# A fused attention and two-layer MoE kernel: token blocks of 512 and 384 in the first MoE layer, and spills of converted weights on POOL's queue

## The chip, the cores and the metric

The kernel runs on one core of a Trainium2 chip. The metric is device time in microseconds (us) of one execution, the median of several runs; lower is better. A core has five engines that run side by side and each work through their own list of instructions in order: TensorE (PE in the profile; its weight loads are shown as PEld), VectorE (DVE), ScalarE (ACT), GpSimd (POOL) and SyncE (SP). SP and POOL also ask for DMA transfers; each does that from its own queue, in the order of its list. Matmuls write to PSUM, eight banks of 512 float32 columns on 128 partitions; everything else lies in SBUF or, if it does not fit, in DRAM.

## What is computed

Softmax attention with a soft cap, then two feed-forward layers over 1792 tokens of width 768. Cut to what matters here:

```python
x = attention(q, k, v, cap)           # 4 x 12 heads x 448 x 64 -> 1792 x 768
h = x @ w_in                          # first layer, 768 x 2048
g = h - np.tanh(h)
y = g @ w_out                         # 2048 x 768
h = y @ w_in2                         # second layer, 768 x 1024
e = np.exp(h - h.max(-1)); solu = h * e / (e.sum(-1) + 1e-9)
out = layer_norm(solu) * g_ln @ w_out2
```

The weights arrive as float64. A weight w is used as a pair of float32r numbers, hi and lo, and so are the activations; a product is three matmuls: hi by hi, hi by lo, lo by hi.

## The kernel before

The tokens are worked on in two halves of 896 (two batches of 448; `hb` 0 and 1). Each half runs attention, then the first MoE layer (`moe1`), then the second (`moe2`). Features lie on partitions and tokens along the free axis, so a half is 896 columns; a PSUM tile has two banks, and the kernel puts 448 columns in each (`hp[:, g, :S]`, g = 0 and 1).

`moe1` has four chunks of 512 hidden features. For each chunk `up` makes four hp tiles of 128 features, from two weight loads of three units; each hp tile takes 6 slices of the input width, 3 products and 2 token groups: 36 matmuls. The very first chunk is made by `first`, which does three of its four tiles group by group (`gg=(g,)`), so that it can begin before the second group's attention is done. `nonlinear` then computes h - tanh(h) on ScalarE and VectorE over all 896 columns: L487, L489, L495, L491 and L501 on ScalarE; L493, L497, L496, L498 and L502 on VectorE. L496 is the last to read hp; L502 makes gl, the lo part of the result. `down` multiplies the chunk with w_out: six op tiles of 24 matmuls (4 slices, 3 products, 2 groups), which are added to `acc` (L524; the first chunk is copied by L522). After the last chunk, L526 and L527 make the hi and lo parts yh and yl, the next layer's input. The order on TensorE is up of chunk c + 1, then down of chunk c. hp and op have two PSUM tiles each, so an hp tile's matmuls wait for L496 of the hp tile two before it, and an op tile's for the add of the op tile two before it.

A weight unit is 128 x 512 weights. In the first half it is loaded as pairs of 32-bit words into one of three `st` buffers (L106, SP's queue), packed by L111, L112 and L113 on VectorE, and split into hi (L119, ScalarE) and lo (L120, or L126 in the second layer, VectorE). The pair stays in one of 13 buffers `w` (and one `wx`) until its matmuls are done. It is also saved to DRAM (`keep`, L136), five units after its conversion, and the second half reads it back (L191, SP's queue; the first 13 by L153 on POOL's) instead of converting again. `keep` is called from `unit`, and at the end of attention and of the second layer's loads for all that are pending.

Attention's order is written out by hand. In the MoE layers a scheduler sets the order on each engine at build time, from priorities and its own estimate of times; once built it is fixed.

Of the kernel before, what the change touches and what calls it, by code (L numbers as in the profile page):

```python
# [9 lines left out]
F32 = mybir.dt.float32  # L10
# [4 lines left out]
ALU = mybir.AluOpType  # L15
# [14 lines left out]
def fused_kernel(ctx, tc, qk_in, v, cap, w1, w2, w3, w4, gln, out):  # L30
    nc = tc.nc
    B, H, S, D = 4, 12, 448, 64
# [6 lines left out]
    NK = DM // P  # L39
    HB = B // 2  # L40
    HT = HB * S
# [7 lines left out]
    NCHUNK = w2.shape[0] // NK  # L49
# [83 lines left out]
    def keep():  # L133
        key, w = pending.pop(0)
        d = drw.tile([P, 2, 512], F32R, name=f"d{key}")
        nc.sync.dma_start(d.bitcast(F32), w.bitcast(F32))  # L136
        saved[key] = d

    ahead = {}
# [307 lines left out]
    def moe1(mp, xh, xl, yh, yl):  # L447
        acc = [mp.tile([P, HT], F32, tag=f"acc{d}", name=f"acc{d}", bufs=1) for d in range(NK)]
        gs = {}
        place.update(pool=(mp, WX1), at=-1)  # L450

        def up_mms(hp, wt, m, k0, k1, gg=(0, 1)):
            ms = slice(m * P, (m + 1) * P)
            for kk in range(k0, k1):
                wh, wl = wt[kk]
                xs = [(xh[kk][:, g * S:(g + 1) * S], xl[kk][:, g * S:(g + 1) * S]) for g in range(2)]
                for i in range(2):
                    for g in gg:
                        nc.tensor.matmul(hp[:, g, :S], wh[:, ms], xs[g][i], start=(kk == 0 and i == 0), stop=False)  # L459
                for g in gg:  # L460
                    nc.tensor.matmul(hp[:, g, :S], wl[:, ms], xs[g][0], start=False, stop=(kk == NK - 1))  # L461

        def first():

            gs[0] = []
            wts = [load_w1(0, 0), load_w1(0, 1)]
            hps = [pst("hp", "ab"[half]) for half in range(2) for _ in range(2)]
            for g, k0, k1 in ((0, 0, NK), (1, 0, 3), (1, 3, 4), (1, 4, 5), (1, 5, 6)):
                for m in range(3):
                    up_mms(hps[m], wts[m // 2], m % 2, k0, k1, (g,))  # L470
                    if k1 == NK and g == 1:
                        nonlinear(0, hps[m])
            up_mms(hps[3], wts[1], 1, 0, NK)
            nonlinear(0, hps[3])

        def up(c, half):
            gs.setdefault(c, [])
            wt = load_w1(c, half)
            for m in range(2):
                hp = pst("hp", "a")  # L480
                up_mms(hp, wt, m, 0, NK)
                nonlinear(c, hp)

        def nonlinear(c, hp):
            h = hp[:, :, :S]
            u = mp.tile([P, 2, S], F32, tag="u", name="u")
            nc.scalar.activation(u, h, AF.Square)  # L487
            t = mp.tile([P, 2, S], F32, tag="t", name="t")
            nc.scalar.activation(t, h, AF.Tanh)  # L489
            mk = mp.tile([P, 2, S], U8, tag="mk", name="mk")  # L490
            nc.scalar.activation(mk, t, AF.Square, scale=TS)  # L491
            gf = mp.tile([P, 2, S], F32, tag="gf", name="gf")
            nc.vector.scalar_tensor_tensor(gf, u, C2, h, ALU.mult, ALU.mult)  # L493
            w = mp.tile([P, 2, S], F32, tag="w", name="w", bufs=1)
            nc.scalar.activation(w, u, AF.Square, bias=gat)  # L495
            nc.vector.tensor_tensor(t, h, t, ALU.subtract)  # L496
            nc.vector.scalar_tensor_tensor(gf, w, GB, gf, ALU.add, ALU.mult)  # L497
            nc.vector.copy_predicated(gf, mk, t)  # L498
            gh = mp.tile([P, 2, S], F32R, tag="gh", name="gh", bufs=6)
            gl = mp.tile([P, 2, S], F32R, tag="gl", name="gl", bufs=6)  # L500
            nc.scalar.copy(gh, gf)  # L501
            nc.vector.tensor_tensor(gl, gf, gh.bitcast(F32), ALU.subtract)  # L502
            gs[c].append((gh, gl))

        def down(c):
            for d in range(NK):
                wt = load_w2(c, d)
                op = pst("op")
                nm = CH // P
                for m in range(nm):  # L510
                    gg = gs[c][m]
                    wh, wl = wt[m]
                    for i in range(2):
                        for g in range(2):
                            nc.tensor.matmul(op[:, g, :S], wh, gg[i][:, g], start=(m == 0 and i == 0), stop=False)  # L515
                    for g in range(2):
                        nc.tensor.matmul(op[:, g, :S], wl, gg[0][:, g], start=False, stop=(m == nm - 1))  # L517
                for g in range(2):
                    cs = slice(g * S, (g + 1) * S)
                    a = acc[d][:, cs]  # L520
                    if c == 0:
                        nc.scalar.copy(a, op[:, g, :S])  # L522
                    else:
                        nc.vector.tensor_tensor(a, op[:, g, :S], a, ALU.add)  # L524
                    if c == NCHUNK - 1:
                        nc.scalar.copy(yh[d][:, cs], a)  # L526
                        nc.vector.tensor_tensor(yl[d][:, cs], a, yh[d][:, cs].bitcast(F32), ALU.subtract)  # L527

        first()
        for c in range(NCHUNK):  # L530
# [151 lines left out]
    for hb in range(2):  # L682
        xh, xl = xtiles()
# [73 lines left out]
```

## Time and profile before

| | |
|---|---|
| Median of 3 runs | 907.37 us (906.84 to 908.77) |
| The profiled execution | 907.26 us, of which the span from first to last instruction is 905.5 us |
| TensorE busy | 897.6 us (99% of the span), 5162 matmuls; weight loads 727.9 us |
| VectorE busy | 613.4 us (68%) |
| ScalarE busy | 416.7 us (46%) |
| GpSimd busy | 48.1 us (5%) |
| DMA | 142.98 MB, mean 158 GB/s; SP's queue 112.95 MB, POOL's 29.20 MB |
| First layer, first half / second half | about 93 to 336 us / about 538 to 780 us |

The granted TensorE clock is 1.00 in every stretch read here. Matmuls are pipelined: the record of one overlaps that of the next, so a group's mean duration is not the time that one adds. That is read from start to start. Shares of the whole span hide that the two halves differ: only the first converts weights.

### The profile page before, as it was taken

How to read it: one execution, taken by the hardware profiler on the slowest of the kernel's cores; microseconds unless marked ns; L12 is line 12 of the kernel's file. 1: busy time of each engine (PE TensorE's matmuls, PEld its weight loads, DVE VectorE, ACT ScalarE, POOL GpSimd, SP SyncE). 2: the span in 40 equal slices, each digit the busy share in tenths (PEclk: the TensorE clock that was granted, in tenths of full speed). 3: DMA queues.
4: the chain of work that ended last, by engine and by line, in shares of the span. 5: the costliest groups of instructions: out<-in, count | busy, mean ns of one | idle time of the engine just before them, and what ended most of it. 6: DMA issues, size and time to landing. Idle time of an engine off the chain costs nothing.

```text
span 905.5 us, 12979 instructions
## 1 busy us (share of the span) xinstructions
PE 897.6 (99%) x5162; PEld 727.9 (80%) x5162; DVE 613.4 (68%) x954; ACT 416.7 (46%) x469; POOL 48.1 (5%) x88
## 2 busy tenths in 40 slices
PE   8999999999999999999999999999999999999998
PEld 5444699999989998888865448999999999888887
DVE  6687989899999990988257985970543634306841
ACT  7999276446254231443279871852512502113311
POOL 2211000000000000001022200000000000000000
PEclk9999999999999999999999999999999999999999
DMA  8554680796875873730256623433242432231301
GB/s 292 183 181 149 229 324 24 237 343 210 268 267 177 320 244 126 255 134 36 102 184 198 209 92 116 134 107 113 73 140 71 138 99 87 70 131 33 128 35 53
DMA packets 46424, 142.98 MB, mean 158 GB/s; under 512 B 10460, under 2 KB 13532, under 8 KB 46364
## 3 DMA queue, kind: packets, MB, share of 16 engines
q1 hardware_dynamic: 39180, 112.95, 36.6%
q0 software_dynamic: 7040, 29.20, 9.4%
q8 instruction: 41, 0.67, 0.3%
q14 instruction: 19, 0.16, 0.1%
q10 hardware_dynamic: 144, 0.00, 0.0%
HBM read 98.64 MB, written 43.33 MB: 157 GB/s over the span
## 4 chain that ended last, share of the span: by engine, by line
PE 84%; DVE 10%; DMA 3%; issue 1%; ACT 1%; SPq 0%; DVEq 0%
PE op L515 14%; PE hp L459 14%; PE op L517 7%; PE hp L461 7%; PE o L307 7%; PE hp L226 4%; PE hp L227 4%; PE hp L225 4%; PE s L275 4%; PE oab L615 2%; PE oab L619 2%; PE oab L616 2%; PE so L324 2%; DMA st<-in_moe_w_out_dram 2%; PE x L281 2%; PE tp L564 1%
## 5 line engine op out<-in xcount | busy, mean ns | idle before, releaser
L459 PE MATMUL hp<-xh,w 128*128 128x448 f32 x384 | 115.8, 368 | 1.5 <-DVE t L496 1.5
L459 PE MATMUL hp<-xl,w 128*128 128x448 f32 x384 | 115.8, 367 | 0.0
L461 PE MATMUL hp<-xh,w 128*128 128x448 f32 x384 | 115.7, 367 | 0.0
L517 PE MATMUL op<-gh,w 128*128 128x448 f32 x336 | 96.4, 367 | 0.0
L515 PE MATMUL op<-gl,w 128*128 128x448 f32 x336 | 96.1, 367 | 0.0
L515 PE MATMUL op<-gh,w 128*128 128x448 f32 x336 | 96.1, 367 | 0.0
L459 PEld LDWEIGHTS hp<-xh,w 128*128 128x128 f32 x384 | 71.8, 188 | 10.5 <-issue 2.5
L461 PEld LDWEIGHTS hp<-xh,w 128*128 128x128 f32 x384 | 72.1, 188 | 7.4 <-issue 0.7
L459 PEld LDWEIGHTS hp<-xl,w 128*128 128x128 f32 x384 | 72.1, 188 | 7.4 <-issue 0.7
L307 PE MATMUL o<-t,vf 128*32 128x448 f32 x768 | 77.8, 542 | 0.0
L299 ACT ACTIVATE t<-t,shift,capt 128x3136 f32<-128x3136 f32 (+2 forms) x26 | 72.8, 2807 | 0.7
L524 DVE TENSOR_TENSOR acc<-op,acc 128x448 f32<-128x448 f32 x72 | 41.9, 619 | 45.7 <-PE op L517 45.7
L515 PEld LDWEIGHTS op<-gl,w 128*128 128x128 f32 x336 | 63.1, 188 | 5.9
L515 PEld LDWEIGHTS op<-gh,w 128*128 128x128 f32 x336 | 63.0, 188 | 5.9
L517 PEld LDWEIGHTS op<-gh,w 128*128 128x128 f32 x336 | 63.1, 188 | 5.8
L292 ACT ACTIVATE t<-s,tscale 128x1344 f32<-128x1344 f32 x48 | 63.5, 1379 | 5.7 <-PE s L275 5.7
L225 PE MATMUL hp<-w,xh 128*128 128x512 f32 x168 | 65.5, 390 | 0.0
L227 PE MATMUL hp<-w,xl 128*128 128x512 f32 x168 | 65.4, 389 | 0.0
L226 PE MATMUL hp<-w,xh 128*128 128x512 f32 x168 | 65.4, 389 | 0.0
L501 ACT CAST gh<-gf 128x896 fp32r<-128x896 f32 x32 | 30.1, 944 | 73.8 <-PE op L517 47.8
L493 DVE SCALAR_TENSOR_TENSOR gf<-u,hp 128x896 f32<-128x896 f32 x32 | 34.8, 1088 | 41.2 <-ACT t L489 41.2
L487 ACT ACTIVATE u<-hp 128x896 f32<-128x896 f32 x32 | 29.5, 922 | 68.3 <-PE hp L461 68.3
(161 smaller groups left out, 1670.6 us busy)
## 6 DMA issues: line engine op xcount, KB each, us to landing
d<-w SPq DMA_DIRECT2D x69, 512.0 KB
w<-d SPq DMA_DIRECT2D x56, 512.0 KB
st<-in_moe_w_out_dram SPq DMA_DIRECT2D x35, 512.0 KB
st<-in_moe_w_in_dram SPq DMA_DIRECT2D x25, 512.0 KB
kq<-in_qk_dram POOLq DMA_DIRECT2D x21, 480.0 KB, 4.0
w<-d POOLq DMA_DIRECT2D x13, 512.0 KB, 5.2
st<-in_moe_w_in_dram POOLq DMA_DIRECT2D x11, 512.0 KB, 5.1
vf<-in_v_dram POOLq DMA_DIRECT2D x22, 256.0 KB, 3.2
```

The source lines that it names most:

```text
L225: nc.tensor.matmul(ps, sh, mh, start=first, stop=False)
L226: nc.tensor.matmul(ps, sh, ml, start=False, stop=False)
L227: nc.tensor.matmul(ps, sl_, mh, start=False, stop=last)
L275: nc.tensor.matmul(s[b // 3][:, b % 3, :S], st[rows, cs], mv[rows, KW:], start=first, stop=last)
L292: nc.scalar.activation(t[:, 3 * half:3 * half + 3], s[half][:, :, :S], AF.Tanh, scale=tscale)
L299: nc.scalar.activation(t[:, sl], t[:, sl], AF.Exp, bias=shift, scale=capt)
L307: nc.tensor.matmul(o[cs, :S], vf[:, r, cs], t[:, 6 if r == 3 else 2 * r + g // 2], start=(r == 0), stop=(r == 3))
L459: nc.tensor.matmul(hp[:, g, :S], wh[:, ms], xs[g][i], start=(kk == 0 and i == 0), stop=False)
L461: nc.tensor.matmul(hp[:, g, :S], wl[:, ms], xs[g][0], start=False, stop=(kk == NK - 1))
L515: nc.tensor.matmul(op[:, g, :S], wh, gg[i][:, g], start=(m == 0 and i == 0), stop=False)
L517: nc.tensor.matmul(op[:, g, :S], wl, gg[0][:, g], start=False, stop=(m == nm - 1))
L524: nc.vector.tensor_tensor(a, op[:, g, :S], a, ALU.add)
```

## The change

Three things change.

In `moe1` the 896 columns of a PSUM tile are filled as one flat row, in a block of 512 (the first bank) and a block of 384 (the second). For each block all slices and products run before the next block begins, where before both groups took turns within each product. `turned` reverses the order of the two blocks at each tile, so that a tile begins with the width with which the tile before it ended. The three group-wise tiles of `first` keep 448 columns. The number of matmuls and their weight loads stays.

Eviction follows: `nonlinear` reads the flat 896 columns, and L524 (now L530), L522, L526 and L527 (now L533) are one instruction of 896 columns instead of two of 448.

`keep` asks for its DMA from POOL's queue instead of SP's.

```diff
--- before.py
+++ after.py
@@ -133,7 +133,7 @@
     def keep():
         key, w = pending.pop(0)
         d = drw.tile([P, 2, 512], F32R, name=f"d{key}")
-        nc.sync.dma_start(d.bitcast(F32), w.bitcast(F32))
+        nc.gpsimd.dma_start(d.bitcast(F32), w.bitcast(F32))
         saved[key] = d
 
     ahead = {}
@@ -449,16 +449,24 @@
         gs = {}
         place.update(pool=(mp, WX1), at=-1)
 
-        def up_mms(hp, wt, m, k0, k1, gg=(0, 1)):
+        blocks = [(0, 512), (512, HT)]
+
+        def turned():
+            blocks.reverse()
+            return list(blocks)
+
+        def flat(ps):
+            return ps.rearrange("p a b -> p (a b)")
+
+        def up_mms(hp, wt, m, k0, k1, gg=None):
             ms = slice(m * P, (m + 1) * P)
-            for kk in range(k0, k1):
-                wh, wl = wt[kk]
-                xs = [(xh[kk][:, g * S:(g + 1) * S], xl[kk][:, g * S:(g + 1) * S]) for g in range(2)]
-                for i in range(2):
-                    for g in gg:
-                        nc.tensor.matmul(hp[:, g, :S], wh[:, ms], xs[g][i], start=(kk == 0 and i == 0), stop=False)
-                for g in gg:
-                    nc.tensor.matmul(hp[:, g, :S], wl[:, ms], xs[g][0], start=False, stop=(kk == NK - 1))
+            parts = [(flat(hp)[:, a:b], slice(a, b)) for a, b in turned()] if gg is None else [(hp[:, g, :S], slice(g * S, (g + 1) * S)) for g in gg]
+            for o, cs in parts:
+                for kk in range(k0, k1):
+                    wh, wl = wt[kk]
+                    nc.tensor.matmul(o, wh[:, ms], xh[kk][:, cs], start=(kk == 0), stop=False)
+                    nc.tensor.matmul(o, wh[:, ms], xl[kk][:, cs], start=False, stop=False)
+                    nc.tensor.matmul(o, wl[:, ms], xh[kk][:, cs], start=False, stop=(kk == NK - 1))
 
         def first():
 
@@ -471,7 +479,7 @@
                     if k1 == NK and g == 1:
                         nonlinear(0, hps[m])
             up_mms(hps[3], wts[1], 1, 0, NK)
-            nonlinear(0, hps[3])
+            nonlinear(0, hps[3], True)
 
         def up(c, half):
             gs.setdefault(c, [])
@@ -479,10 +487,10 @@
             for m in range(2):
                 hp = pst("hp", "a")
                 up_mms(hp, wt, m, 0, NK)
-                nonlinear(c, hp)
-
-        def nonlinear(c, hp):
-            h = hp[:, :, :S]
+                nonlinear(c, hp, True)
+
+        def nonlinear(c, hp, whole=False):
+            h = flat(hp)[:, :HT].rearrange("p (a b) -> p a b", a=2) if whole else hp[:, :, :S]
             u = mp.tile([P, 2, S], F32, tag="u", name="u")
             nc.scalar.activation(u, h, AF.Square)
             t = mp.tile([P, 2, S], F32, tag="t", name="t")
@@ -507,24 +515,22 @@
                 wt = load_w2(c, d)
                 op = pst("op")
                 nm = CH // P
-                for m in range(nm):
-                    gg = gs[c][m]
-                    wh, wl = wt[m]
-                    for i in range(2):
-                        for g in range(2):
-                            nc.tensor.matmul(op[:, g, :S], wh, gg[i][:, g], start=(m == 0 and i == 0), stop=False)
-                    for g in range(2):
-                        nc.tensor.matmul(op[:, g, :S], wl, gg[0][:, g], start=False, stop=(m == nm - 1))
-                for g in range(2):
-                    cs = slice(g * S, (g + 1) * S)
-                    a = acc[d][:, cs]
-                    if c == 0:
-                        nc.scalar.copy(a, op[:, g, :S])
-                    else:
-                        nc.vector.tensor_tensor(a, op[:, g, :S], a, ALU.add)
-                    if c == NCHUNK - 1:
-                        nc.scalar.copy(yh[d][:, cs], a)
-                        nc.vector.tensor_tensor(yl[d][:, cs], a, yh[d][:, cs].bitcast(F32), ALU.subtract)
+                fo = flat(op)
+                for a, b in turned():
+                    for m in range(nm):
+                        gh, gl = (flat(g)[:, a:b] for g in gs[c][m])
+                        wh, wl = wt[m]
+                        nc.tensor.matmul(fo[:, a:b], wh, gh, start=(m == 0), stop=False)
+                        nc.tensor.matmul(fo[:, a:b], wh, gl, start=False, stop=False)
+                        nc.tensor.matmul(fo[:, a:b], wl, gh, start=False, stop=(m == nm - 1))
+                a = acc[d]
+                if c == 0:
+                    nc.scalar.copy(a, fo[:, :HT])
+                else:
+                    nc.vector.tensor_tensor(a, fo[:, :HT], a, ALU.add)
+                if c == NCHUNK - 1:
+                    nc.scalar.copy(yh[d], a)
+                    nc.vector.tensor_tensor(yl[d], a, yh[d].bitcast(F32), ALU.subtract)
 
         first()
         for c in range(NCHUNK):
```

On TensorE, in the first half's second hp tile of `up` (hp_1505; xh and xl are the input slices, w the weights), the last two slices before:

```order
L459 MATMUL hp_1505<-xl_104,w_913 128x448 x2
L461 MATMUL hp_1505<-xh_98,w_913 128x448 x2
L459 MATMUL hp_1505<-xh_99,w_913 128x448 x2
L459 MATMUL hp_1505<-xl_105,w_913 128x448 x2
L461 MATMUL hp_1505<-xh_99,w_913 128x448 x2
L459 MATMUL hp_1559<-xh_94,w_737 128x448 x2
```

and the end of the first block and the beginning of the second now:

```order
L467 MATMUL hp_1505<-xh_99,w_913 128x512
L468 MATMUL hp_1505<-xl_105,w_913 128x512
L469 MATMUL hp_1505<-xh_99,w_913 128x512
L467 MATMUL hp_1505<-xh_94,w_737 128x384
L468 MATMUL hp_1505<-xl_100,w_737 128x384
L469 MATMUL hp_1505<-xh_94,w_737 128x384
```

The pairs of 448 (x2) have become runs of 18 at 512 and 18 at 384 columns, each over all six slices.

The scheduler also orders VectorE anew. Ahead of the ninth hp tile's nonlinear steps (L493 and L496, now L501 and L504; L111 to L120 are pieces of weight conversions), before:

```order
L111 TENSOR_SCALAR f<-st 128x512
L112 SCALAR_TENSOR_TENSOR f<-st,f 128x512
L113 SCALAR_TENSOR_TENSOR f<-st,f 128x512
L120 TENSOR_TENSOR w<-f,w 128x512
L111 TENSOR_SCALAR f<-st 128x512
L112 SCALAR_TENSOR_TENSOR f<-st,f 128x512
L113 SCALAR_TENSOR_TENSOR f<-st,f 128x512
L493 SCALAR_TENSOR_TENSOR gf<-u,hp 128x896
L497 SCALAR_TENSOR_TENSOR gf<-w,gf 128x896
L496 TENSOR_TENSOR t<-hp,t 128x896
```

and now:

```order
L120 TENSOR_TENSOR w<-f,w 128x512
L111 TENSOR_SCALAR f<-st 128x512
L120 TENSOR_TENSOR w<-f,w 128x512
L112 SCALAR_TENSOR_TENSOR f<-st,f 128x512
L111 TENSOR_SCALAR f<-st 128x512
L113 SCALAR_TENSOR_TENSOR f<-st,f 128x512
L112 SCALAR_TENSOR_TENSOR f<-st,f 128x512
L501 SCALAR_TENSOR_TENSOR gf<-u,hp 128x896
L113 SCALAR_TENSOR_TENSOR f<-st,f 128x512
L504 TENSOR_TENSOR t<-hp,t 128x896
```

A further L120 has moved in front, and L113 stands between L501 and L504, with L497 (now L505) behind it.

On POOL, at the end of the first half's weight conversions, where rstd is a step of the second layer's norm and kq and vf are the next half's attention inputs, before:

```order
L106 DMA st<-in_moe_w_out_dram 128x1024
L243 DMA kq<-in_qk_dram 128x960 x3
L249 DMA vf<-in_v_dram 128x512
L560 TENSOR_TENSOR rstd<-rstd,mhalf 128x1 x7
L243 DMA kq<-in_qk_dram 128x960
```

and now:

```order
L136 DMA d_1_5_3684<-w 128x1024
L136 DMA d_0_3697<-w 128x1024
L243 DMA kq<-in_qk_dram 128x960 x3
L249 DMA vf<-in_v_dram 128x512
L136 DMA d_1_3708<-w 128x1024
L136 DMA d_1_3719<-w 128x1024
L136 DMA d_2_3732<-w 128x1024
L136 DMA d_3_3743<-w 128x1024
L136 DMA d_3_3754<-w 128x1024
L136 DMA d_4_3767<-w 128x1024
L566 TENSOR_TENSOR rstd<-rstd,mhalf 128x1 x2
L136 DMA d_5_3769<-w 128x1024
```

The spills of the second layer's units (d with a number) stand in front of the loads of the next half and between the norm's steps; before, they stood in SP's queue between the loads of weights.

## Rows read from the trace of the kernel before

**Rows 1.** Busy time by stretch: PE, PEld, DVE, ACT, POOL (records), clock, DMA share, GB/s.

```profile
122.20:202.60 80.40, 80.40 (x393) 73.28 (x392) 75.80 (x99) 51.06 (x70) 0.00 (x0) 1.00 0.62 210
202.60:307.00 104.40, 102.86 (x507) 94.59 (x506) 100.69 (x155) 45.77 (x60) 0.00 (x0) 1.00 0.71 245
562.00:779.90 217.90, 217.90 (x1056) 197.90 (x1055) 110.75 (x124) 82.18 (x102) 0.00 (x0) 1.00 0.33 108
```

**Rows 2.** Timeline of PE: start, us to the end of the group, operands, shapes, count.

```profile
603.85 0.57 PE L515 MATMUL op<-gh,w 128*128 128x448 f32 x2
...
607.57 0.57 PE L515 MATMUL op<-gh,wx 128*128 128x448 f32 x2
...
329.84 0.57 PE L517 MATMUL op<-gh,w 128*128 128x448 f32 x2
...
335.92 0.57 PE L517 MATMUL op<-gh,w 128*128 128x448 f32 x2
...
345.18 0.39 PE L225 MATMUL hp<-w,xh 128*128 128x512 f32 x1
...
347.90 0.39 PE L225 MATMUL hp<-w,xh 128*128 128x512 f32 x1
...
453.17 0.28 PE L225 MATMUL ob<-w,lhz 128*128 128x256 f32 x1
...
455.21 0.28 PE L227 MATMUL ob<-w,llz 128*128 128x256 f32 x1
...
779.93 0.40 PE L225 MATMUL hp<-w,xh 128*128 128x512 f32 x1
...
782.02 0.39 PE L225 MATMUL hp<-w,xh 128*128 128x512 f32 x1
```

**Rows 3.** Waits for us in total, times, longest; then timelines of DVE and PE.

```profile
PE hp L459 <- DVE t L496: 1.5, 2, 1.3
...
201.63 1.08 DVE L496 TENSOR_TENSOR t<-hp,t 128x896 f32<-128x896 f32 x1
...
202.96 0.57 PE L459 MATMUL hp<-xh,w 128*128 128x448 f32 x2
...
261.53 1.08 DVE L496 TENSOR_TENSOR t<-hp,t 128x896 f32<-128x896 f32 x1
...
262.76 0.65 PE L459 MATMUL hp<-xh,w 128*128 128x448 f32 x2 [1.25 <-DVE t L496]
...
306.05 2.08 DVE L502 TENSOR_TENSOR gl<-gf,gh 128x896 fp32r<-128x896 f32 x2
...
307.14 0.57 PE L515 MATMUL op<-gh,w 128*128 128x448 f32 x2
```

**Rows 4.** Timeline of DVE in the first half's first layer.

```profile
248.68 1.15 DVE L524 TENSOR_TENSOR acc<-op,acc 128x448 f32<-128x448 f32 x2
...
250.41 1.28 DVE L112 SCALAR_TENSOR_TENSOR f<-st,f 128x512 uint32<-128x512 uint32 x2
251.62 1.28 DVE L113 SCALAR_TENSOR_TENSOR f<-st,f 128x512 uint32<-128x512 uint32 x2
252.82 0.42 DVE L111 TENSOR_SCALAR f<-st 128x512 uint32<-128x512 uint32 x1
253.16 0.69 DVE L120 TENSOR_TENSOR wx<-f,wx 128x512 fp32r<-128x512 f32 x1
253.76 0.68 DVE L120 TENSOR_TENSOR w<-f,w 128x512 fp32r<-128x512 f32 x1
```

**Rows 5.** Timeline of SP's queue and DVE; then DVE's waits for landings, first half.

```profile
252.33 0.93 SPq L106 DMA_DIRECT2D st<-in_moe_w_out_dram  x2
...
257.40 0.43 DVE L111 TENSOR_SCALAR f<-st 128x512 uint32<-128x512 uint32 x1 [1.62 <-DMA st<-in_moe_w_out_dram]
...
DVE f L111 <- DMA st<-in_moe_w_out_dram: 4.4, 4, 1.6
...
DVE f L111 <- DMA st<-in_moe_w_in_dram: 1.8, 3, 1.0
```

## The prediction

> **What bounds the kernel now.** I read the busy time by stage first. In the first layer of the second half (562 to 779.9 us) TensorE is busy all the time and VectorE half of it; in the first half VectorE is busy 75.8 of 80.4 us and then 100.7 of 104.4 us, and TensorE is without work for 1.54 us of the second of these stretches [rows 1]. So the second half is bound by TensorE alone; in the first, which also converts the weights, the two run side by side with a few per cent between them. A change of matmul widths has to be costed apart in each.
>
> The second view is the timeline of the matmuls, for start to start, since records overlap [rows 2]. At 448 columns 18 matmuls take 3.72 us in the second half, 206.7 ns each, and 30 take 6.08 us late in the first half, 202.7 ns each: two steady paces for one shape. At 512 columns 12 take 2.72 us, 226.7 ns; at 256 columns 17 take 2.04 us, 120.0 ns. From 256 to 512 that is 106.7 ns for 256 columns, 0.417 ns a column, and 13.3 ns fixed. On that line 448 would be 200.0 ns: it lies 2.7 or 6.7 ns above.
>
> The third view is who waits for whom [rows 3]. In the first half TensorE waits twice, 1.5 us in all, for L496, the last reader of an hp tile in PSUM: the ninth one ends at 202.71 (201.63 + 1.08) and the tile that reuses its banks starts at 202.96; the thirteenth ends at 262.61 and its successor starts at 262.76 after 1.25 us. The sixteenth gl is ready at 308.13; the down product that needs it starts at 307.14 and uses it after 18 matmuls, about 311: 2.9 us to spare. VectorE is the one to watch there, and its order is fixed when the program is built.
>
> **The widths, second half.** Per half, 13 hp tiles of 18 pairs and 24 op tiles of 12 pairs change: 522 pairs. (In first(), three tiles keep 448.) A pair costs 413.4 ns. 384 columns occur nowhere in the trace. The line gives 173.3 ns; with the excess of 448 it would be 176.0 or 180.0 ns. Cheaper than the line is excluded by all three measured widths. I take 173.3, because 256 and 512, its two neighbours in multiples of 128, lie on the line: pair 400.0, saved 13.4 x 522 = 7.0 us; with 180.0, 3.5 us. Each tile now has one change of width (the turning order avoids the second): 37 in the half. The one entry into 512 that I can read, at 779.93, costs 2.09 us for nine steps against 2.04, 0.05 us [rows 2]; 37 of 0 to 0.05 make 0 to 1.9 us; I take 0.7, as that entry also changed operands. Net: 6.3 us saved.
>
> **The widths, first half.** If TensorE alone decided, 522 pairs at 5.4 to 13.4 would save 2.8 to 7.0 us. I take 4.0, as the fast pace is seen there, and subtract 0.7: 3.3, plus at most 1.5 of waits that may vanish.
>
> **VectorE's new order, first half.** This is the term with the other sign. The order of the changed program puts pieces of weight conversions ahead of the steps that TensorE waits for. Steps start to start [rows 4]: L111 0.34 us (252.82 to 253.16), L112 and L113 0.60 (1.21 and 1.20 for two), L120 0.60; an 896-wide step 1.00 (2.08 for two less 1.08 for one, [rows 3]); two 448-wide adds 1.15 against 1.08 for one of 896, 0.07 saved for each tile. Counted from the first L493 of the layer, the orders differ so:
> up to the ninth L496: L111 14 to 15, L112 14 to 15, L113 14 to 16, L120 14 to 15, L497 9 to 8: 0.34 + 0.60 + 1.20 + 0.60 - 1.00 = +1.7 us;
> up to the thirteenth: L112 28 to 29, L113 28 to 30, L120 27 to 28, 12 half adds to 6 whole ones: 0.60 + 1.20 + 0.60 - 6 x 0.07 = +2.0 us;
> up to the sixteenth gl: L111 and L112 38 to 40, L113 38 to 41, L120 38 to 39, 22 half adds to 11: 0.68 + 1.20 + 1.80 + 0.60 - 0.77 = +3.5 us.
> VectorE has next to no free time there, so these steps come that much later, while TensorE arrives earlier. The fifteenth hp tile then starts at 262.6 + 2.0 = 264.6. Two tiles of 36 at 200 ns and six of 24 bring TensorE to 264.6 + 14.4 + 28.8 = 307.8. In the new loop a block needs the fourth gl after 9 matmuls instead of 18, at 309.7; VectorE has it at 308.1 + 3.5 = 311.6: a new wait of 1.9 us. The remaining 135 matmuls take 27.0 us: the stage ends at 338.6 instead of 336.3, **2.3 us later**, although its matmuls are shorter.
>
> **Eviction in one piece.** Add, copy to yh and subtraction to yl now wait for the whole tile instead of overlapping by halves: about half a step, 0.6 us, later at the end of the layer. The next stage's 16th matmul needs it, 15 x 0.227 = 3.4 us in; three whole steps are 3.2 us. So 0 to 0.6 us in each half; I take 0.2 for both together. Behind it on VectorE only conversions of weights that the next stage uses much later are queued.
>
> **Spills on POOL's queue.** What this could free on SP is the start of the weight loads. It has nothing to free: the load at 252.33 is issued as soon as the buffer is read out, at 251.62 + 0.68 = 252.30 [rows 4, 5]. Loads are held by their three buffers, not by spills in front of them. What remains is their time on the way: VectorE waits 4.4 + 1.8 us for landings in this layer, up to 1.62 us at a time [rows 5]. Both kinds share the engines before and after, so I put this at 0, with bounds of -6 (all waits gone) and +6 us (doubled). Today a load stands behind spills in one queue. The Trainium skill, DMA: Bandwidth & Descriptors, section Queues, rings and completion order, says each engine takes turns between the queue rows that have work; by it a load would pass part of a spill. No run shows it yet; it bears on the chance of the second case below. On POOL the spills stand in front of rstd's power and of the next half's kq loads, and each waits for its conversion; by the new VectorE order these conversions come before the step that feeds the power, so I cost it 0.
>
> **Sum**, against the profiled execution's 907.3 us (median of the runs 907.4): 907.3 - 6.3 + 2.3 + 0.2 + 0 = **903.5 us**.
>
> **Rivals.**
> *VectorE gets out of the way.* If loads land earlier, the 6.2 us of waits cover the 3.5 us of added work, and the first half is bound by TensorE: 3.3 + 1.5 saved instead of 2.3 lost. 907.3 - 6.3 - 4.8 + 0.2 = 896.4. For it: separate queues; against it: conversions are issued earlier, so they ask for data earlier too.
> *384 is as odd as 448.* At 180.0 ns the second half saves 3.5 - 0.7 = 2.8: 907.3 - 2.8 + 2.3 + 0.2 = 907.0.
> *Widths only share out the same time.* If 384 carried 13.3 ns more than the line, 186.7, the pair would cost 413.4 as now: 907.3 + 0.7 + 2.3 + 0.2 = 910.5. The Trainium skill, TensorE: Matmul & The Clock Gate, section Back-to-back issue gap, gives columns over 2.4 plus a fixed 2.5 ns, by which 512 + 384 costs what 448 + 448 costs and nothing is gained. The trace agrees on the slope; its fixed part is 13.3 ns and 448 does not fit it.
> *Spills crowd the loads: slower.* If a load shares the engines with up to eight spills that POOL has out, and VectorE's waits double, the first half ends another 6.2 us later: 909.7. It decides from 3.9 us of added waits on, where the sum reaches 907.4.
>
> **Chances.** Forecast 0.50 (its own range 901 to 905.5), VectorE free 0.20, odd 384 0.14, shared-out widths 0.06, crowded loads 0.10. A measurement of this kernel can tell 0.2%, 1.8 us, from no change: faster below 905.6, slower above 909.2. Faster: most of the first case and the second, 0.68; same: its rest, the third and some of the fifth, 0.20; slower: the fourth and most of the fifth, 0.12. The range 896 to 907.5 leaves out the last two and little more.
>
> **What would show it.** Second half: pairs of 400 ns (24 matmuls of an op tile in 4.8 us), the layer some 6 us shorter with no new idle time. First half: TensorE waiting for the ninth and thirteenth last reader of hp (some 3 us each) and for the sixteenth gl, the layer ending 2 us later than now. Wrong if TensorE's waits there vanish (second case), if 384 columns come at more than 176 ns (third, fourth), or if VectorE's waits for landings grow beyond 10 us (fifth).

## The result and the profile after

The changed kernel takes 916.3 us (median of 6 runs, 915.2 to 917.2) against 907.1 us for the kernel before (901.8 to 910.3): the ratio is 1.0113, 95% interval 1.0086 to 1.0140. It is 1.1% slower; 903.5 us and faster had been forecast. The profiled execution took 915.2 us, 913.4 us of it span, at a mean granted clock of 0.996.

Where the 7.9 us of span went is read best by layers. The view is busy time by stretch, columns as in [rows 1]. Each stretch runs from the first matmul of the first MoE layer to the first of the second: the upper row is the first half of the tokens, the lower the second half. The first fence is the kernel before, the second the changed one.

```profile
92.90:336.30 243.40, 241.82 (x1204) 218.01 (x1201) 231.99 (x354) 112.76 (x154) 0.00 (x0) 1.00 0.70 242
536.70:779.90 243.20, 243.20 (x1196) 217.66 (x1193) 127.50 (x152) 84.65 (x103) 0.00 (x0) 1.00 0.32 106
```

```profile
92.90:350.60 257.70, 243.54 (x1205) 213.27 (x1202) 231.54 (x332) 111.96 (x143) 29.73 (x51) 0.99 0.62 219
550.60:787.90 237.30, 237.30 (x1197) 210.58 (x1194) 126.05 (x130) 83.19 (x92) 0.00 (x0) 1.00 0.33 109
```

The layer of the second half is 5.9 us shorter, TensorE busy all the time. That of the first half is 14.3 us longer. VectorE has no more work in it than before (231.5 against 232.0 us); TensorE is without work for 14.2 us (257.7 - 243.54), where it was 1.6. The rest of the program is half a microsecond shorter.

The waits of the first half say what TensorE waits for. The view is waits from 90 to 352 us: us in total, times, longest. Before there were 1.5 us of TensorE for L496, which is L504 now [rows 3], and 4.4 and 1.8 us of VectorE for landings [rows 5].

```profile
PE hp L467 <- DVE t L504: 9.1, 3, 5.0
PE op L524 <- DVE gl L510: 2.0, 1, 2.0
PE hp L467 <- DVE xh L387: 1.8, 1, 1.8
PE op L523 <- DVE acc L530: 1.1, 1, 1.1
...
DVE f L111 <- DMA st<-in_moe_w_out_dram: 9.6, 7, 2.2
DVE f L111 <- DMA st<-in_moe_w_in_dram: 5.8, 4, 3.4
...
DVE rs L361 <- DMA rs<-su: 4.2, 1, 4.2
```

TensorE waits for VectorE, and VectorE waits for DMA: 15.4 us for landings of weight words, where it was 6.2, and 4.2 us for the softmax sums at the end of attention, which is new. One such chain in the timeline of all engines (start, duration, engine, operands, idle before and its cause):

```profile
205.18 0.39 PE L469 MATMUL hp<-xh,w 128*128 128x512 f32 x1
...
206.20 0.43 DVE L111 TENSOR_SCALAR f<-st 128x512 uint32<-128x512 uint32 x1 [1.53 <-DMA st<-in_moe_w_in_dram]
...
209.34 1.08 DVE L504 TENSOR_TENSOR t<-hp,t 128x896 f32<-128x896 f32 x1
...
210.57 0.77 PE L467 MATMUL hp<-xh,w 128*128 128x512 f32 x1 [5.01 <-DVE t L504]
```

VectorE stands 1.53 us at a conversion of weights that is queued ahead of the last reader of hp (L504); TensorE then has no free hp tile in PSUM for 5.01 us. The 1.53 us are only the last piece: from 105 to 206.5 us VectorE's waits for landings add up to 7.8 us, where before they were 2.8. The load that answers to the one in [rows 5], in the same view:

```profile
249.84 0.76 POOL L136 DMA_DIRECT2D d<-w  x1 [5.01 <-DVE w L120]
...
250.17 2.60 SPq L106 DMA_DIRECT2D st<-in_moe_w_out_dram  x2
...
256.55 0.43 DVE L111 TENSOR_SCALAR f<-st 128x512 uint32<-128x512 uint32 x1 [2.19 <-DMA st<-in_moe_w_out_dram]
```

A spill is issued at 249.84, the load at 250.17, and its words are used 6.38 us later, where it was 5.07 us in [rows 5].

### The profile page after: what moved, and what is told of

Same layout as the page of the kernel before. It is cut to its first block, busy times and chain, and to the rows that moved or that the text cites. A ratio compares the mean times of both kernels' runs of the same rounds, so it can differ in the third digit from the quotient of the medians.

```text
span 913.4 us, 12956 instructions
## 1 busy us (share of the span) xinstructions
PE 892.8 (98%) x5162; PEld 716.0 (78%) x5162; DVE 610.9 (67%) x906; ACT 414.0 (45%) x445; POOL 89.8 (10%) x160
## 4 chain that ended last, share of the span: by engine, by line
PE 68%; DVE 18%; DMA 8%; issue 4%; ACT 2%; SPq 0%; DVEq 0%; ACTq 0%
PE o L307 6%; PE op L524 5%; PE op L525 5%; PE op L523 5%; PE hp L469 4%; PE hp L467 4%; PE hp L468 4%; PE hp L226 4%; PE hp L227 4%; PE hp L225 4%; PE s L275 4%; DMA st<-in_moe_w_out_dram 3%; PE oab L621 2%; DMA st<-in_moe_w_in_dram 2%; PE oab L625 2%
## 5 line engine op out<-in xcount | busy, mean ns | idle before, releaser
L467 PE MATMUL hp<-xh,w 128*128 128x512 f32 (+2 forms) x384 | 140.3, 366 | 10.9 <-DVE t L504 9.1
L469 PE MATMUL hp<-xh,w 128*128 128x512 f32 (+2 forms) x384 | 140.2, 365 | 0.0
L468 PE MATMUL hp<-xl,w 128*128 128x512 f32 (+2 forms) x384 | 140.1, 365 | 0.0
L524 PE MATMUL op<-gl,w 128*128 128x512 f32 (+1 forms) x336 | 122.8, 366 | 2.1 <-DVE gl L510 2.0
L523 PE MATMUL op<-gh,w 128*128 128x512 f32 (+1 forms) x336 | 122.5, 365 | 1.1 <-DVE acc L530 1.1
L525 PE MATMUL op<-gh,w 128*128 128x512 f32 (+1 forms) x336 | 122.8, 365 | 0.0
L467 PEld LDWEIGHTS hp<-xh,w 128*128 128x128 f32 x384 | 72.4, 189 | 21.4 <-issue 11.2
L524 PEld LDWEIGHTS op<-gl,w 128*128 128x128 f32 x336 | 63.6, 189 | 10.0 <-DVE gl L510 2.9
L530 DVE TENSOR_TENSOR acc<-op,acc 128x896 f32<-128x896 f32 x36 | 39.2, 1089 | 43.5 <-PE op L525 43.5
L119 ACT CAST w<-f 128x512 fp32r<-128x512 f32 x44 | 27.1, 622 | 89.5 <-DVE f L113 62.8
L136 POOL DMA_DIRECT2D d<-w x69 | 40.3, 584 | 270.8 <-DVE w L120 195.9
```

Of the source, the lines that this page charges most:

```text
L467: nc.tensor.matmul(o, wh[:, ms], xh[kk][:, cs], start=(kk == 0), stop=False)
L468: nc.tensor.matmul(o, wh[:, ms], xl[kk][:, cs], start=False, stop=False)
L469: nc.tensor.matmul(o, wl[:, ms], xh[kk][:, cs], start=False, stop=(kk == NK - 1))
L523: nc.tensor.matmul(fo[:, a:b], wh, gh, start=(m == 0), stop=False)
L524: nc.tensor.matmul(fo[:, a:b], wh, gl, start=False, stop=False)
L525: nc.tensor.matmul(fo[:, a:b], wl, gh, start=False, stop=(m == nm - 1))
```

## The experiments

**Two causes apart.** Theory Q says that the spills on POOL's queue cost the first half its time; theory B that the blocks do. The first run puts the spills back on SP:

```diff
-        nc.gpsimd.dma_start(d.bitcast(F32), w.bitcast(F32))
+        nc.sync.dma_start(d.bitcast(F32), w.bitcast(F32))
```

> The changed kernel with the spills put back on SP's queue, so only the blocks of 512 and 384 are left. Theory Q (spills on POOL's queue cost the first half its 14 us, by crowding the loads and by the order that VectorE gets): first half back at 336 or up to 3 us under it, second half 6 us shorter as in the changed kernel, 898 to 901.5 us; VectorE's order up to the ninth and thirteenth last reader of hp is that of the kernel before, its landing waits about 6 us. Theory B (the blocks cost it, by needing the fourth gl after 9 matmuls and by the whole-tile eviction): first half still ends 10 us late or more, 911 to 916 us, and TensorE's waits for VectorE stay.

The second makes the reverse edit of this line in the kernel before.

> The kernel before with only the spills moved to POOL's queue. Theory Q: first half some 10 to 14 us longer, second half unchanged at 243 us, 917 to 921 us; landing waits of VectorE in the first layer near 15 us. Theory B: 906 to 909 us. If only VectorE's new order counted (its counts up to the ninth and thirteenth last reader are those of the changed kernel) and not the transfers, 2 to 4 us slower, 909 to 911.

Measured: blocks alone 904.1 us, ratio 0.9972 (0.9952 to 0.9993); spills alone 916.0 us, ratio 1.0105 (1.0080 to 1.0130). The spills alone make all of the loss. The first half's layer with the blocks alone, by stretch:

```profile
92.90:339.40 246.50, 241.81 (x1205) 211.91 (x1202) 231.45 (x332) 111.53 (x143) 0.00 (x0) 0.99 0.71 240
```

and VectorE's waits for landings there:

```profile
DVE f L111 <- DMA st<-in_moe_w_out_dram: 5.6, 7, 2.0
DVE f L111 <- DMA st<-in_moe_w_in_dram: 3.2, 4, 1.6
```

The layer is 11.2 us shorter than with the spills on POOL, VectorE's waits for landings at 8.8 us and none for the softmax sums. 15.4 + 4.2 - 8.8 = 10.8 us of waits less: nearly the whole difference. Q expected 898 to 901.5 us for the blocks alone and missed: what it did not foresee is that this layer is still 3.1 us longer than before, not shorter, in this one execution.

**Which spills.** Thirteen spills stand at the end of attention; the others belong to the MoE layers. `keep` gets its queue as an argument:

```diff
-    def keep():
+    def keep(eng=nc.gpsimd):
...
         while pending:
-            keep()
+            keep(nc.sync)
```

> The changed kernel with the thirteen spills at the end of attention on SP's queue again, those of the first layer still on POOL's. If the early spills are the harm (they start at 80 us instead of 105 and stand in the way of the softmax sums' transfer and of the first weight loads): most of the 14 us comes back, 901 to 906. If those of the layer itself are: 911 to 915, landing waits still over 10 us.

The reverse has SP as the default and POOL for the thirteen.

> The reverse: the thirteen spills at the end of attention on POOL's queue, those of the first layer on SP's. If the early spills are the harm: 911 to 916, with the 2.2 us gap of TensorE at 110 us and the wait of VectorE for the softmax sums. If those of the layer itself are: 901 to 905, with that gap alone left.

Measured: 916.9 us (1.0114, 1.0090 to 1.0138) and 908.4 us (1.0018, 1.0000 to 1.0036). The second is above the 901 to 905 expected. So the layers' own spills are most of the harm: with them on POOL's queue, first layer 258.5 us, waits for landings 9.1 + 8.2 us. The early ones add 3.3 us to the blocks alone (249.8 against 246.5), by a wait that they bring back, the second of these of VectorE:

```profile
DVE f L111 <- DMA st<-in_moe_w_out_dram: 5.0, 4, 2.0
DVE rs L361 <- DMA rs<-su: 4.0, 1, 4.0
DVE f L111 <- DMA st<-in_moe_w_in_dram: 2.9, 3, 1.3
```

How that comes about is in the timeline of the changed kernel: seven spills of 512 KB issued from 80.44 us on, the transfer of the sums (3.5 KB) at 87.59 behind them in time, its reader on VectorE at 98.81.

```profile
80.44 3.90 POOL L136 DMA_DIRECT2D d<-w  x7
...
87.59 1.13 SPq L357 DMA_DIRECT2D rs<-su  x1
...
98.81 0.23 DVE L361 SCALAR_TENSOR_TENSOR rs<-rs,gcol 56x16 f32<-56x16 f32 x1 [4.23 <-DMA rs<-su]
```

The two parts don't add: 3.3 and 12.0 us apart, 11.2 together.

**Bytes or order.** Moving the spills also gave VectorE another order, the one that the prediction costed at 2.3 us. This run keeps every order and takes the bytes away:

```diff
-        d = drw.tile([P, 2, 512], F32R, name=f"d{key}")
-        nc.gpsimd.dma_start(d.bitcast(F32), w.bitcast(F32))
-        saved[key] = d
+        d = drw.tile([P, 2, 512], F32R, name=f"d{key}"); n = 32 if saved else 512
+        nc.gpsimd.dma_start(d.bitcast(F32)[:, :, :n], w.bitcast(F32)[:, :, :n])
+        saved[key] = next(iter(saved.values()), d)
```

> The changed kernel with every spill after the first cut to a sixteenth of its bytes (32 of 512 columns), still on POOL's queue; the second half reads the first spilled tile in place of each, so all its transfers stay, but its weights are not the right ones. All orders on TensorE, VectorE and ScalarE are those of the changed kernel, to the row. Theory C (the spills' bytes crowd the loads and the softmax sums): VectorE's landing waits fall from 15.4 to about 6 us or less, its 4.2 us wait for the softmax sums goes, the first layer of the first half takes 243 to 247 us instead of 257.7, the whole 901 to 905. Theory O (VectorE's new order is what delays TensorE): the first layer stays at 254 to 258 us, the whole at 912 to 916.

Measured: 898.2 us, ratio 0.9921 (0.9890 to 0.9951). The layer by stretch:

```profile
93.00:332.70 239.70, 239.62 (x1204) 211.06 (x1201) 231.35 (x332) 111.96 (x143) 36.22 (x51) 1.00 0.41 122
```

and all of VectorE's waits for DMA in it:

```profile
DVE f L111 <- DMA st<-in_moe_w_out_dram: 1.0, 2, 0.6
DVE f L111 <- DMA st<-in_moe_w_in_dram: 0.6, 2, 0.4
```

VectorE, ScalarE and POOL have the same orders from the first row to the last, POOL issues as many DMAs, and the layer is 18.0 us shorter. TensorE waits for nothing in this stretch. Theory O falls: VectorE's new order delays nobody as long as its words are there. The ninth last reader of hp starts at 199.7 us here, at 209.3 in the changed kernel and at 201.6 before. The DMA share is 0.41 instead of 0.62. A spill also holds its buffer until it has landed, but the profile puts no wait of the changed kernel down to the landing of a spill.

The same in the kernel before, with 448 columns throughout, prices the widths in the first half:

> The kernel before with every spill after the first cut to a sixteenth of its bytes, on POOL's queue (the second half reads the first spilled tile in place of each, so its weights are not the right ones). With the bytes gone, TensorE should set the first half's first layer with either width, and its length tells the widths' gain there: 448 columns at 202.7 ns throughout 242 us against the 239.75 of the blocks, at 206.7 ns throughout 246. If the widths gain nothing there: 240 us. VectorE's landing waits under 2 us.

Measured: 903.6 us, ratio 0.9965 (0.9941 to 0.9989); first layer 240.2 us, 448 columns at 202.7 ns throughout. The blocks took 239.7: the widths are worth about half a microsecond there, not 3.3. But the traced execution was the fastest of its ten, 899.8 us of 899.8 to 906.0, while the six with blocks lie within 897.5 and 899.0. By the ratios (0.9965 and 0.9921, with intervals of about 0.003 either way) the widths are worth some 4 us over both halves, so other executions probably lose more to 448 columns than this one.

**The blocks' own parts.** Eviction by halves again, in the loops with blocks and with spills on SP:

```diff
-                a = acc[d]
+                for g in range(2):
+                    cs = slice(g * S, (g + 1) * S)
+                    a = acc[d][:, cs]
...
-                    nc.vector.tensor_tensor(a, fo[:, :HT], a, ALU.add)
+                        nc.vector.tensor_tensor(a, fo[:, cs], a, ALU.add)
```

> Blocks alone (spills on SP), with the down product's results added and split by halves of 448 again. The blocks alone left the first layer of the first half 3.1 us longer than before. If the eviction in one piece is why (fewer steps of VectorE between two conversions, so loads have less time to land): 243 to 244 us there, 900 to 902 in all. If the order of the blocks or the widths are why: 246 to 247 us, 903 to 905.

The next has the old loops for `hb == 0` and blocks for `hb == 1` only.

> Spills on SP, the old loops in the first half, blocks and eviction in one piece in the second half alone. VectorE's order in the first half is that of the kernel before, to the row counts. All theories: first layer of the first half 243.4 us as before, that of the second half 237.3 instead of 243.2, so 6 us under the kernel before, 900 to 902 us; ratio 0.993 to 0.9945. If the first half did gain from the shorter matmuls somewhere, this one would be no faster than the blocks alone (904).

Measured: 903.0 us (0.9983, 0.9963 to 1.0004), first layer 246.1 us; and 902.2 us (0.9971, 0.9953 to 0.9989), first layer 242.8 us. The eviction is not what costs the first half. In the medians blocks in both halves and in the second alone are the same (0.9972, 0.9971), so the 3.1 us of the one trace above are not established as a cost. What surprised is the second run: it lacks 5.9 us in the second half's layer by its trace, but its median is only 2.9 us under the kernel before. Hence one more trace of the kernel before, unchanged:

> The kernel before, unchanged, for a second trace. In the first trace 448 columns came at 206.7 ns from 560 us to the end of the layer, in that of the spills alone at 202.7 ns up to some 595 us and at 206.7 after. If the pace is a matter of the single execution: another split, the first layer of the second half between 239 (all at 202.7) and 243.2 us (all at 206.7). If it is fixed by the program: 206.7 from 560 us on again, 243.2 us.

The median is 906.9 us, among the 905.0 to 907.1 of the other rounds, but in this trace the layer of the second half takes 238.9 us, not 243.2. The views are busy time by stretch and the timeline of matmuls, counterpart of the first two rows of [rows 2]:

```profile
538.00:776.90 238.90, 238.90 (x1197) 217.70 (x1194) 127.51 (x152) 84.53 (x103) 0.00 (x0) 1.00 0.34 108
...
602.97 0.57 PE L515 MATMUL op<-gh,w 128*128 128x448 f32 x2
...
607.43 0.57 PE L517 MATMUL op<-gh,wx 128*128 128x448 f32 x2
```

22 matmuls in 4.46 us, 202.7 ns each, where the first trace has 206.7 at the same place. The pace of 448 columns is a matter of the single execution. The trace of the spills alone has both within this layer: 12 matmuls in 2.43 us at one place and 24 in 4.96 at the other.

```profile
574.99 0.57 PE L459 MATMUL hp<-xh,w 128*128 128x448 f32 x2
...
577.42 0.56 PE L459 MATMUL hp<-xh,w 128*128 128x448 f32 x2
...
639.89 0.57 PE L517 MATMUL op<-gh,w 128*128 128x448 f32 x2
...
644.85 0.57 PE L461 MATMUL hp<-xh,w 128*128 128x448 f32 x2
```

Against this second trace of before the blocks save 1.6 us in the second half (238.9 to 237.3), against the first 5.9.

**Another second queue.** The same line with `nc.scalar` in place of `nc.gpsimd`:

> The changed kernel with the spills on ScalarE's queue instead of POOL's: a second queue beside SP's, but not POOL's own. If two queues side by side are the harm (a spill and a load then share the engines instead of following one another): 911 to 917 us, landing waits over 12 us. If it is POOL's kind of queue: 902 to 906. ScalarE waits for each conversion that it spills, which may add some us in either case; its waits will tell.

Measured: 916.6 us, ratio 1.0124 (1.0094 to 1.0155), waits for landings 7.0 + 6.3 us. So it isn't POOL's kind of queue alone. The run is not clean: ScalarE waits itself (8.3 us at once for a spill to land), and the stretch between the two first layers grew by 6.7 us.

**Fewer spills.** If the bytes are the trouble, some weights could go unspilled and be converted a second time:

```diff
+            place["n"] = place.get("n", 0) + 1
+            if key in again or (key[0] in "12" and len(again) * 2 < place["n"]):
+                again.add(key)
+                return hi, lo
             pending.append((key, w))
```

> Blocks with spills on SP, but every second weight unit that the first layer of the first half converts itself is not spilled (18 of 35): the second half loads the raw words and converts it again, the same 512 KB and some 2.1 us of VectorE each. If the spills' bytes decide the first half (theory C): landing waits of VectorE near half of the 8.8 us, the layer 242 to 244 us instead of 246.5. The second half stays at 237 to 238 us if VectorE's free half takes the 38 us of conversions: 897 to 901 in all. If its conversions come late there, TensorE waits for them and the whole is 903 or more.

For none at all the condition is `key in again or key[0] in "12"`.

> The same with none of the 35 units spilled. Theory C: first half as with small spills, 239.5 to 241 us. Second half: VectorE has some 118 us of work there and gets 74 more, 192 of 237; if it keeps up 896 to 900 in all, if loads and conversions come too late for TensorE the second half grows past 245 us and the whole past 904.

Measured: 908.2 us (1.0022, 1.0000 to 1.0043) and 908.8 us (1.0020, 0.9995 to 1.0046): both misses. With half of the spills the waits for landings were 10.1 us, no fewer than with all, and the first layer took 249.0 us. With none they were 5.9 us, the first layer 243.6 us. VectorE's order changed in both, so bytes and order are mixed here. In the second half VectorE's doubled work was carried with half (237.4 us) but not quite with none (241.2 us, TensorE waiting 1.9 us at once). What this refuted is that bytes alone set the waits.

**The lead of the loads.** A load is issued when one of the three buffers `st` has been read out, and is needed when VectorE comes round to it. A fourth buffer makes that lead longer and leaves all traffic. For its room, the fourteenth slot for converted weights goes:

```diff
-    WA, WX1, WX2 = 13, 1, 0
+    WA, WX1, WX2 = 13, 0, 0
...
-        st = sp.tile([P, 512, 2], U32, tag="st", name="st", bufs=3)
+        st = sp.tile([P, 512, 2], U32, tag="st", name="st", bufs=4)
```

> Blocks with spills on SP, and four landing buffers st for raw words instead of three; to make room the fourteenth slot for converted weights (wx) goes. If the lead that three buffers give a load (issued when one is read out, needed 4 to 7 us later) is what turns a load's time into VectorE's waits: landing waits from 8.8 to under 3 us, first layer of the first half 240 to 242 us, 897 to 900 in all. If the waits come from the DMA engines' throughput: they stay at 7 us or more and the whole at 902 to 905.

> The control: blocks with spills on SP, three landing buffers as before, the fourteenth slot gone. Within 2 us of the blocks alone (902 to 906), or slower where a conversion has to wait for a slot.

> The changed kernel (spills on POOL's queue) with four landing buffers and without the fourteenth slot. Lead theory: a load may take its 6 to 7 us without a wait; landing waits from 15.4 to under 5 us, first layer of the first half 243 to 247 us (the 4.2 us at the softmax sums stay), 901 to 906 in all instead of 916. Throughput theory: waits stay over 10 us, 912 to 917.

> Blocks in the second half alone, spills on SP, four landing buffers, without the fourteenth slot. Lead theory: first layer of the first half 240 to 241 us with 448 columns too (the kernel before without the spills' bytes took 240.2), second half 237.3, 897 to 900 in all. Beside the run with blocks in both halves it tells once more what the widths are worth in the first half: under 1 us.

Measured, in this order: 897.2 us (0.9903, 0.9871 to 0.9934); the control without the fourth buffer 901.0 us (0.9950, 0.9929 to 0.9971); spills on POOL 907.1 us (1.0008, 0.9989 to 1.0027); blocks in the second half only 898.8 us (0.9930, 0.9906 to 0.9955). The layer of the first half in the first of them, by stretch:

```profile
93.30:332.30 239.00, 238.94 (x1204) 211.15 (x1201) 230.99 (x332) 111.64 (x143) 0.00 (x0) 1.00 0.69 247
```

and its only wait for a landing:

```profile
DVE f L111 <- DMA st<-in_moe_w_out_dram: 0.9, 1, 0.9
```

The DMA share is 0.69, against 0.70 in the kernel before: throughput was not short, lead was. On POOL's queue, too, the fourth buffer takes the waits for landings from 15.4 to 4.9 us, but the wait for the sums doubled, and the layer took 249.3 us instead of the 243 to 247 expected. VectorE's waits for the sums and for landings there:

```profile
DVE rs L361 <- DMA rs<-su: 8.8, 1, 8.8
...
DVE f L111 <- DMA st<-in_moe_w_out_dram: 2.8, 5, 1.2
...
DVE f L111 <- DMA st<-in_moe_w_in_dram: 2.1, 1, 2.1
```

The first of these kernels beats both the kernel before and the changed one: blocks in both halves, spills on SP, four landing buffers. Its gain over the kernel before is 0.97%, of which the control without the fourth buffer has half. That half was not expected (901.0 us against 902 to 906): VectorE still waits 7.3 us for landings there, and why giving up the fourteenth slot helps is open.

One table puts the runs together (us; from the profiled executions but the ratio). "Load" is the mean time from the issue of a load to its use, over those loads for which VectorE stood idle by more than a quarter of a microsecond, with their count; it is worked out from the two timelines as in [rows 5]. It compares late loads only, and few of them.

| kernel | ratio | first layer, first half | waits for landings | for the sums | load |
|---|---|---|---|---|---|
| before | 1 | 243.4 | 6.2 | 0 | 5.2 (6) |
| blocks alone | 0.9972 | 246.5 | 8.8 | 0 | 5.4 (8) |
| spills on POOL alone | 1.0105 | 255.0 | 11.2 | 4.2 | 6.0 (7) |
| both: the change | 1.0113 | 257.7 | 15.4 | 4.2 | 6.0 (10) |
| same, hardly any spill bytes | 0.9921 | 239.7 | 1.6 | 0 | 4.6 (3) |
| spills on ScalarE's queue | 1.0124 | 253.6 | 13.3 | 0 | 6.0 (10) |
| blocks, four landing buffers | 0.9903 | 239.0 | 0.9 | 0 | 5.8 (1) |
| the change, four landing buffers | 1.0008 | 249.3 | 4.9 | 8.8 | 6.3 (5) |

## Why the prediction was wrong, point by point

**The widths, second half: right for the execution it was read from.** Forecast 6.3 us, the traces give 5.9. 384 columns come at 173.5 ns, on the line, and 512 at 226.7 as before, so the rivals of an odd 384 and of widths that only share out the time are out. The rows, from the timeline of matmuls, span 23 steps of 384 and 9 of 512:

```profile
606.88 0.33 PE L467 MATMUL hp<-xh,w 128*128 128x384 f32 x1
...
610.87 0.33 PE L469 MATMUL hp<-xh,w 128*128 128x384 f32 x1
...
778.68 0.39 PE L525 MATMUL op<-gh,w 128*128 128x512 f32 x1
...
780.72 0.39 PE L525 MATMUL op<-gh,w 128*128 128x512 f32 x1
```

The weak step is another: 206.7 ns was taken for the pace of 448 columns in the second half, although [rows 2] had both paces. The second trace shows 202.7 there, and by that the term is 1.6 us. For a median it should lie between; the ratios of the blocks in the second half alone (0.9971, 2.6 us) agree.

**The widths, first half.** 3.3 us forecast if TensorE alone decided; with the bytes gone it does, and 240.2 against 239.7 us leave 0.5. With four landing buffers it is 240.3 against 239.0, 1.3 us. By the pitches, 522 pairs at 5.4 ns make 2.8 us, less what 37 changes of width cost; the fast pace held through the layer in these traces, so the 4.0 us of the prediction were too many for them.

**VectorE's new order: 2.3 us forecast, nothing found.** This term fell. The counts of conversion steps up to the ninth and thirteenth last reader and the sixteenth gl are the same in the run with hardly any spill bytes, and TensorE waits for none of them. The prediction added the steps to a VectorE that it took to be full; 6.2 of its 11.4 idle us in that layer were waits for landings, and the added steps fit when these are gone. The waits it named did appear in the changed kernel (9.1 us for last readers, 2.0 for a gl), from another cause.

**Eviction in one piece.** 0.2 us forecast; by halves the ratio is 0.9983 against 0.9972, which doesn't tell them apart.

**Spills on POOL's queue: the step that failed.** It was put at 0 with bounds of 6 us; it is 11.2 us of the first layer (257.7 against 246.5). The measured 916.3 us are 12.8 above the forecast 903.5, and most of that is here. Two things were missed. First, the prediction asked only whether a load is issued later, saw that it is not, and took the time on the way as shared either way. The row was there: a load issued at 252.33 and used at 257.40 with 1.62 us of wait had 3.45 us of lead [rows 5], so each further microsecond on the way is one of VectorE's, and in part of TensorE's. Second, at the end of attention nobody looked at POOL: on SP the spills stood behind attention's own transfers (they began at 105 us), on POOL they start at 80.44 and meet the softmax sums.

Starved loads took 6.0 us with spills on a second queue, 5.2 to 5.4 with the spills in SP's own, 4.6 with hardly any. Of the 47 loads of the changed kernel's first layer after 122 us, 14 are issued within 1 us after a spill; of the 46 of before, 5; but of the 46 with the spills on ScalarE's queue only 7, and those loads were as slow, so this nearness alone doesn't explain it. The DMA packets in the microsecond from 255.50 to 256.50 us, in which the load issued at 250.17 is on its way (queue: packets, MB, share of 16 engines; q0 is POOL's, q1 SP's):

```profile
q0 software_dynamic: 56, 0.22, 52.8%
q1 hardware_dynamic: 53, 0.20, 50.9%
```

The spills had half of what was moved while VectorE waited for that load. The Trainium skill, DMA: Bandwidth & Descriptors, section Queues, rings and completion order, says that an engine takes turns between the queues that have work. The prediction drew from it that a load could pass part of a spill. The longer loads and these packets agree better with its other side, that a spill on its own queue takes turns with the loads too; the turns of a single engine are not shown.

**The sum for the first half** closes within a microsecond. TensorE's waits are 9.1 + 2.0 + 1.8 + 1.1 = 14.0 us, 12.5 more than before. Its clock cost about 3.2: it was at 0.57 for stretches of 3.5 and 4.0 us (rows in the last section), where before it was 1.00. The shorter matmuls gave back 0.5 to 1.3 by the pairs of runs above. 12.5 + 3.2 less these is 14.4 to 15.2 us; the layer grew by 14.3.

**The rivals.** The fifth, spills that crowd the loads, was the right mechanism, with a chance of 0.10 and a price of 6.2 us. The waits for landings rose from 6.2 to 15.4 us, past the 10 us named as its sign; that is 9.2 us more where it priced 6.2, and the sums and the clock came on top. The first rival, VectorE out of the way, is what a fourth landing buffer brings, in another kernel, with the spills on SP: 897.2 us, near the 896.4 computed for it.

Left open: why half of the spills on SP made as many waits as all of them, why the kernel is faster without the fourteenth slot, and whether the 3.1 us that the blocks alone show in the first half of one trace are more than scatter.

## What to carry to other kernels

Before a write-back is moved to a queue of its own, read from the trace how long a load has between its issue and its use, and how much of that it needs: if an engine already waits for landings, the lead is gone, and whatever makes a load slower is paid for. A shared queue can be the cheaper one: with the blocks, writes in the loads' own queue left VectorE 8.8 us of waits for landings, in a queue beside it 15.4 and 4.2 for the sums. And a time per instruction read from one execution should be looked up in a second one before hundreds of them are added up.

## What the runs showed of the hardware

448 columns have two steady paces, 202.7 and 206.7 ns, and the same program shows one or the other at the same place in two executions, while 256, 384 and 512 columns lie on one line where they were read: 120.0, 173.5 and 226.7 ns. Why is not settled. The two executions may be of different chips, but the trace of the spills alone has both paces within one layer.

After a wait TensorE's granted clock can fall. In the changed kernel it idled from 205.57 to 210.57 us; the first two rows are the time just after and the 16 us that follow, the third comes after the layer's last two waits (busy time by stretch, the clock is the third value from the end):

```profile
210.50:214.00 3.50, 3.43 (x9) 2.79 (x10) 3.50 (x6) 1.30 (x3) 0.56 (x2) 0.57 0.80 296
214.00:230.00 16.00, 16.00 (x82) 14.39 (x81) 16.00 (x22) 11.26 (x15) 1.56 (x3) 1.00 0.44 159
322.50:326.50 4.00, 4.00 (x15) 3.91 (x14) 0.64 (x1) 0.00 (x0) 0.00 (x0) 0.57 0.62 250
```

0.57 is a stretch spent mostly at the lower level of 1.2 GHz, after which it is back at 2.4. So a wait of 5.0 us cost about 6.5 (3.5 us at 0.57 lose 1.5); the 4.0 us of the third row lose 1.7. Not every wait does it: after the 2.28 us up to 272.43 the clock stayed at 1.00. With hardly any spill bytes, or with four landing buffers and blocks in both halves, there are no such waits, and the mean clock of the whole execution is 1.000.
